# Half of w_out loaded as float32 over SyncE's queue and cast on the chip, with a new order of first loads

## The chip, the core and the metric

The kernel runs on one core of one Trainium2 chip. A core has five engines that work at the same time, each from its own list of instructions: TensorE (PE in the profile; its weight loads are shown as PEld), VectorE (DVE), ScalarE (ACT), GpSimd (POOL) and SyncE (SP). Transfers between the main memory and the on-chip memory (SBUF) are issued by POOL and SP and carried out by 16 DMA engines. Matmul results go to a second on-chip memory, PSUM, and have to be copied out by DVE or ACT.

The metric is the device time of one launch in microseconds (us). The time before is 254.22 us, the median of three runs (253.74, 254.22 and 254.31).

## What is computed

```python
# attention inside chunks of 64 tokens: q, k, v are [8, 8, 576, 64], float32
scores = (q_c @ k_c.T) / sqrt(64)
scores = scores - max(scores)
attn = exp(scores) / (sum(exp(scores)) + 1e-9)
x = (attn @ v_c)                 # put back to [4608, 512]
# feed-forward: w1, w2 [512, 1024], w3 [1024, 1024], w_out [1024, 512], float32
h = ((x @ w1) * (x @ w2)) @ w3
out = h @ w_out                  # [4608, 512], float32
```

## The kernel before

All matmuls are in bfloat16; the inputs are float32 in main memory, and POOL's DMAs cast them while they are loaded. Since no nonlinearity stands between w3 and w_out, the kernel first computes the product w3o = w3 @ w_out on the chip and then applies it as one matrix.

**Groups.** The 4608 tokens are 36 groups of 128 tokens, two chunks each. For a group, q and k are loaded for all heads (`load_qk`, line 264, tile `raw`), transposed (line 317 on PE for groups 0 to 11, line 321 as a DMA transpose on SP's queue, tile `kqT`, for groups 12 to 35), and copied to `kT` and `qd`. Then come the scores (line 345, tile `p_sc`), maximum, subtraction, exponential, sum and normalisation (lines 353 to 371, tiles `nm`, `sd`, `e`, `ss`, `an`), the transpose of the weights (line 376 on PE for groups 0 to 15, line 327 on SP's queue, tile `at`, for the rest), and attn @ v (line 387, tile `p_av`), which is copied into the x tile `xt`. v is loaded for each of the 8 batches (line 270, two DMAs, tile `vd`); a batch has 9 chunks, so that group 4 is the first to need batch 1.

**w3o.** For each of 8 row blocks of w3 (`load_w3`, line 291; shown as `w_sb`): 8 transposes (line 428), a copy (`w3t`), and 8 matmuls with w_out (line 439) in as many pieces as w_out is loaded in: here two halves, blocks 0 to 3 and 4 to 7 (`load_wo`, line 298, tile `wo_sb`). `wo_cut` holds the pieces, `wo_got` what each piece waits for.

**Feed-forward.** Nine tiles of 4 groups (512 tokens). For each of 8 blocks j, 4 matmuls with w1 and 4 with w2 (line 471, `w12` loads at line 282), a copy (`a_sb`) and a product (`abT`); then for each group 8 matmuls with w3o (line 502), a copy to an output row block, and a store on SP's queue (line 512). The first 12 output row blocks reuse the memory of w3 and w_out, the others take the 20 buffers of `o_sb`.

**What sets the order.** The order of instructions on every engine is made when the kernel is built. Each piece of work is an `Op` with the engines that may do it, a planned cost, a key (smaller goes first), what it must come after, and the buffers that it takes and frees. `Plan.run` steps through planned time: whenever an engine is free, it gets the ready op with the smallest key. POOL is the exception: it takes its loads in the order in which they were added, which at the start is the list `LOADS`. ('qk', g) is q and k of group g, ('w3', 7, 8) a row block of w3, ('wo', 4, 8) half of w_out, ('v', 0, 0, 2) v of batch 0, ('w12', 0, 2) the columns for blocks 0 and 1, and ('ident',) the identity matrix that every transpose on PE needs and that POOL makes. For a transfer the plan holds the issuing engine for `issue`, then shares the DMA engines between the first transfers of POOL's and SP's rings, and lets it land `lag` later. So planned costs, planned start times (`free`, `flown`) and lags change no instruction by themselves, but they decide the order on all engines. On the chip the engines wait for each other by semaphores, in that order.

Up to the first `p_av` that isn't a filler, PE gets matmuls on zeros (line 563) where the plan has gaps; 14 of them stand at the very start.

Of the kernel before, what the change touches and what calls it, by code (L numbers as in the profile page):

```python
# [10 lines left out]
ACT = mybir.ActivationFunctionType  # L11
# [3 lines left out]

LOADS = [('wo', 0, 4), ('qk', 1), ('qk', 0), ('ident',), ('w3', 7, 8), ('wo', 4, 8), ('w3', 6, 7), ('qk', 2),
# [3 lines left out]
TILES = [4] * 9  # L22
XT = 16
OUT_AFTER, OUT_KEY = 35, 80
QK_BY_DMA, A_BY_DMA = set(range(12, 36)), set(range(16, 36))

# [18 lines left out]
class Plan:  # L45
# [21 lines left out]

    def run(self):
        free = {e: 0.0 for e in ("PE", "ACT", "DVE", "POOL", "SP")}
        free["POOL"] = free["SP"] = 1.2  # L70
        todo = {e: [] for e in free}
        for i, o in enumerate(self.ops):
            o.place, o.left, o.since = i, len(set(map(id, o.after))), 0.0
# [5 lines left out]
                for e in o.engines:  # L79
                    todo[e].append(o)  # L80

        rings, flown = {"POOL": [], "SP": []}, 3.4
        left, now, order, ends = len(self.ops), 0.0, [], [1.2]
        loads = [o for o in self.ops if "POOL" in o.engines]

        def ended(o):
# [21 lines left out]
        while left or any(rings.values()):  # L108
# [13 lines left out]
            for eng in free:  # L122
                if free[eng] > now or len(rings.get(eng, ())) >= self.RING:
                    continue
                pick = [o for o in (loads[:1] if eng == "POOL" else todo[eng]) if ready(o)]
                if not pick:
                    continue
                o = min(pick, key=lambda o: (o.key, o.place))
                for e in o.engines:
                    todo[e].remove(o)  # L130
                if eng == "POOL":
                    loads.pop(0)
                o.start, o.engine = now, eng
                cost = o.cost[o.engines.index(eng)] if isinstance(o.cost, tuple) else o.cost
                if o.issue:
                    free[eng] = now + o.issue
                    rings[eng].append([free[eng], cost, o])
                else:
                    free[eng] = now + cost
                    o.end = now + cost + o.lag  # L140
                    ended(o)
                for n in o.takes:
                    self.taken[n].append(o)
                order.append(o)
                heapq.heappush(ends, free[eng])
                left -= 1
            while ends and ends[0] <= now:
                heapq.heappop(ends)
# [8 lines left out]
def kernel(  # L157
# [109 lines left out]
    def load_v(b, y0, y1):  # L267
        for t in range(2):
            def emit(eng, t=t):
                nc.gpsimd.dma_start(vds[b % len(vds)][halves[t], 2 * y0:2 * y1, :, t * D:(t + 1) * D].rearrange("p m c d -> p (m c) d"),  # L270
                                    v[b, NM * t + 2 * y0:NM * t + 2 * y1].rearrange("h (c p) d -> p (h c) d", p=C))
            o = load(1.025 * (y1 - y0), 0.5 + 0.335 * (y1 - y0), emit, takes=() if b in v_first else ("vd",),
                     after=(zero_v[b % len(vds)],))
            v_first.setdefault(b, o)
            for y in range(y0, y1):
                v_got.setdefault((b, y), []).append(o)

    def load_w12(j0, j1):
        for dst, w in ((w1_sb, moe_w1), (w2_sb, moe_w2)):
            for t in range(2):  # L280
                def emit(eng, dst=dst, w=w, t=t):
                    nc.gpsimd.dma_start(
                        dst[halves[t], :, j0 * P:j1 * P],
                        w[t * NM * D:(t + 1) * NM * D, j0 * P:j1 * P].rearrange("(m d) n -> d m n", d=D))
                o = load(0.41 * (j1 - j0), 0.62, emit)
        for j in range(j0, j1):
            w12_got[j] = o

    def load_w3(k0, k1):
        def emit(eng):  # L290
            nc.gpsimd.dma_start(w3_sb[:, k0:k1, :], moe_w3.rearrange("(ko p) n -> p ko n", p=P)[:, k0:k1, :])
        o = load(1.45 * (k1 - k0), 0.75, emit)
        for i in range(k0, k1):
            w3_got[i] = o

    def load_wo(k0, k1):
        def emit(eng):
            nc.gpsimd.dma_start(wo_sb[:, k0:k1, :], moe_w_out.rearrange("(ko p) n -> p ko n", p=P)[:, k0:k1, :])
        wo_got.append(load(0.72 * (k1 - k0), 0.75, emit))
        wo_cut.append((k0, k1))  # L300


    x_done = {}

# [117 lines left out]
    def add_w3o(ko, key):  # L422
# [24 lines left out]
        tcp = plan.add(("DVE", "ACT"), (0.7, 1.1), key, tr_copy, after=(tr,), takes=("w3t",), uses=[(tr, "ffn")])  # L447
        mms = []
        for i, (k0, k1) in enumerate(wo_cut):
            mms.append(plan.add("PE", 0.216 * (k1 - k0), key - 0.1 * i, mm_emit(i), after=[tcp, wo_got[i]] + mms,  # L450
                                takes=() if i else ("ffn",), uses=[(tcp, "w3t")], lag=0.2))
        w3o_done.append(plan.add(("ACT", "DVE"), 0.7, key, mm_copy, after=mms, uses=[(mms[0], "ffn")]))

# [69 lines left out]


    made_ident, landing = None, 1.6
    for what, *args in LOADS:
        if what == "ident":
            made_ident = plan.add("POOL", 0.6, 0, lambda eng: make_identity(nc, ident[:]), lag=0.3)
# [67 lines left out]
```

## Time and profile before

| | us |
|---|---|
| median of three runs | 254.22 (253.74 to 254.31) |
| the profiled execution, its own time | 252.69 |
| its span in the profile | 250.9 |
| PE / DVE / ACT / POOL busy | 242.0 / 178.1 / 140.2 / 102.1 |
| POOL's DMA queue | 19.41 MB in 118688 packets |
| SP's DMA queue | 18.36 MB in 41696 packets |

The profile is of one execution, whose own time stands above beside its span; the span leaves out 1.8 us around it. Times in its views count from the span's start. A row of the timeline gives start, duration, engine, line of the kernel, operation, the tile written and the tiles read, and how many instructions it merges; what stands in brackets is the time that the engine was idle before it, and what ended that. DMA rows give the time that the issue took on the engine; when the data had landed is told by a separate line of the view of one source line, in us from the issue. A row of the chain of waits has start, time on the chain, engine, tile and line. A row of the windows has the stretch, its length, the busy time of PE, PEld, DVE, ACT and POOL with counts, the granted PE clock, the DMA engines' share and GB/s. SP's rows are named SPq. MB in DMA rows are bytes written, so a load that casts counts half of what it reads.

### The profile page before, as it was taken

To read this page: it belongs to the slowest core of one execution; us is meant where nothing else is said; L and a number is where in the kernel's file an instruction comes from. 1 tells how busy PE (TensorE), PEld (TensorE's weight loads), DVE (VectorE), ACT (ScalarE), POOL (GpSimd) and SP (SyncE) were. 2 spreads that over 40 slices of the span, in tenths; PEclk is the share of its full clock that TensorE was granted. 3 is DMA by queue.
4 is the path that set the end of the run, shared out by engine and by line. 5 is a ranking of instruction groups with operands and counts; after the bars stand their busy time and mean duration, and the time that the engine had idled before them with its cause. 6 is when DMAs were issued, how large, how long until landed. Compare 5 with 4: busy or idle time off the path is not lost.

```text
span 250.9 us, 4705 instructions
## 1 busy us (share of the span) xinstructions
PE 242.0 (96%) x1771; PEld 124.8 (50%) x1771; DVE 178.1 (71%) x324; ACT 140.2 (56%) x237; POOL 102.1 (41%) x128
## 2 busy tenths in 40 slices
PE   8699989999999999999999999999999999999994
PEld 2356555555655555554544544554454444444443
DVE  6088866888998898788989888888898762232320
ACT  8057465557877786775546556555565344323222
POOL 8847398987529674347414631720000000000000
PEclk9899999999999999999999999999999999999999
DMA  5999999999999999999999999999998992121114
GB/s 79 170 194 190 158 177 180 172 135 144 125 130 154 145 157 133 157 159 126 157 133 155 156 139 157 141 148 151 125 199 280 357 384 80 42 84 42 43 44 167
DMA packets 160406, 38.06 MB, mean 152 GB/s; under 512 B 149376, under 2 KB 154880, under 8 KB 160384
## 3 DMA queue, kind: packets, MB, share of 16 engines
q0 software_dynamic: 118688, 19.41, 119.5%
q1 hardware_dynamic: 41696, 18.36, 40.0%
q8 instruction: 14, 0.23, 0.4%
q14 instruction: 8, 0.07, 0.1%
HBM read 38.80 MB, written 9.44 MB: 192 GB/s over the span
## 4 chain that ended last, share of the span: by engine, by line
PE 87%; DMA 6%; DVE 3%; ACT 2%; issue 1%; POOL 1%; ACTq 0%; POOLq 0%
PE ffn L471 46%; PE ffn L502 23%; PE ffn L439 5%; DMA at<-an 4%; PE p_sc L345 3%; PE p_av L387 3%; DMA raw<-in_k_dram 2%; PE ffn L317 2%; PE p_av L563 1%; PE ffn L376 1%; PE ffn L428 1%; DVE qd L228 1%; ACT kT L226 1%; DVE xt L228 0%; ACT qd L226 0%
## 5 line engine op out<-in xcount | busy, mean ns | idle before, releaser
L471 PE MATMUL ffn<-xt,w_sb 128*128 128x512 bf16 x576 | 134.5, 379 | 0.0
L471 PEld LDWEIGHTS <-w_sb 128*128 128x128 bf16 x576 | 53.6, 98 | 57.6
L480 DVE TENSOR_TENSOR abT<-a_sb,ffn 128x512 bf16<-128x512 f32 x72 | 48.7, 678 | 30.2 <-PE ffn L471 29.6
L502 PE MATMUL ffn<-w3o_sb,abT 128*128 128x512 bf16 (+2 forms) x304 | 67.6, 368 | 0.0
L226 ACT COPY a_sb<-ffn 128x512 f32<-128x512 f32 x72 | 42.0, 584 | 35.7 <-PE ffn L471 35.3
L264 POOL DMA_DIRECT2D raw<-in_q_dram x40 | 34.3, 858 | 31.4 <-DMA kqT<-raw 11.8
L502 PEld LDWEIGHTS <-abT 128*128 128x128 bf16 x304 | 28.4, 98 | 30.5
L264 POOL DMA_DIRECT2D raw<-in_k_dram x40 | 34.3, 859 | 20.8 <-DMA vd<-in_v_dram 10.8
L365 DVE TENSOR_REDUCE ss<-e 128x8 f32<-128x520 bf16 x36 | 24.8, 689 | 5.1 <-ACT e L361 4.8
L361 ACT ACTIVATE e<-sd 128x512 bf16<-128x512 f32 x36 | 22.8, 634 | 7.2 <-DVE sd L357 6.9
L353 DVE TENSOR_REDUCE nm<-p_sc 128x8 f32<-128x512 f32 x36 | 24.3, 675 | 2.4 <-PE p_sc L345 2.3
L226 ACT COPY qd<-kqT 64x512 bf16<-64x512 bf16 x34 | 20.9, 615 | 7.0 <-DMA kqT<-raw 6.7
L357 DVE TENSOR_TENSOR sd<-p_sc,nm 128x512 f32<-128x512 f32 x36 | 24.6, 684 | 0.3
L371 DVE TENSOR_TENSOR an<-e,rs 128x512 bf16<-128x512 bf16 x36 | 24.6, 684 | 0.2
L226 ACT COPY o_sb<-ffn 128x512 f32<-128x512 f32 (+2 forms) x16 | 8.5, 532 | 24.1 <-PE ffn L502 24.0
L270 POOL DMA_DIRECT2D vd<-in_v_dram x16 | 18.5, 1166 | 4.9 <-DMA raw<-in_q_dram 1.7
L226 ACT CAST xt<-p_av 128x512 bf16<-128x512 f32 x24 | 14.0, 585 | 9.3 <-PE p_av L387 9.2
L387 PEld LDWEIGHTS <-vd 128*128 128x128 bf16 x288 | 12.9, 98 | 8.5 <-issue 1.4
L439 PE MATMUL ffn<-wo_sb,w3t 128*128 128x512 bf16 x64 | 15.6, 379 | 0.4 <-DVE w3t L228 0.3
L387 PE MATMUL p_av<-at,vd 128*128 128x64 bf16 x288 | 14.3, 193 | 0.8 <-DVE xt L228 0.7
L345 PEld LDWEIGHTS <-qd 128*128 128x128 bf16 x288 | 12.2, 98 | 5.6 <-ACT qd L226 1.0
L228 DVE COPY qd<-ffn 64x512 bf16<-64x512 bf16 x14 | 5.9, 419 | 10.4 <-ACT kT L226 10.2
(44 smaller groups left out, 160.9 us busy)
## 6 DMA issues: line engine op xcount, KB each, us to landing
out_dram<-o_sb SPq DMA_DIRECT2D x23, 256.0 KB, 2.7
vd<-in_v_dram POOLq DMA_DIRECT2D x16, 288.0 KB, 12.1
raw<-in_q_dram POOLq DMA_DIRECT2D x32, 128.0 KB, 10.0
raw<-in_k_dram POOLq DMA_DIRECT2D x32, 128.0 KB, 9.5
w_sb<-in_moe_w_dram POOLq DMA_DIRECT2D x8, 256.0 KB, 8.8
w_sb<-in_moe_w_dram POOLq DMA_DIRECT2D x16, 128.0 KB, 4.9
out_dram<-w_sb SPq DMA_DIRECT2D x8, 256.0 KB, 3.0
wo_sb<-in_moe_w_out_dram POOLq DMA_DIRECT2D x2, 512.0 KB, 7.1
```

The source lines that it names most:

```text
L226: nc.scalar.copy(o, i)
L264: nc.gpsimd.dma_start(box["t"][r, w], src[b, :, c * C:(c + n) * C, :].rearrange("h p d -> p h d"))
L353: nc.vector.tensor_reduce(nm[:, :, 0], flat(box["sc"]), axis=AX.X, op=ALU.max)
L357: nc.vector.tensor_sub(sd[:], flat(box["sc"]), box["nm"].to_broadcast([P, 8, C]))
L361: nc.scalar.activation(e[:, :, :C], box["sd"][:], ACT.Exp, scale=scale)
L365: nc.vector.reduce_sum(ss[:], box["e"][:], axis=AX.X)
L371: nc.vector.tensor_mul(an[:], box["e"][:, :, :C], box["rs"].to_broadcast([P, 8, C]))
L387: nc.tensor.matmul(t[:, m, cc, :], vds[b % len(vds)][:, m, c, :], box["at"][:, 2 * cc + y, u * C:(u + 1) * C], start=True, stop=True)
L439: nc.tensor.matmul(box["wp"][:], box["t"][:, ki, :], wo_sb[:, ki, :], start=(ki == wo_cut[0][0]), stop=(ki == wo_cut[-1][1] - 1))
L471: nc.tensor.matmul(t[:, :w], wt[:, ki, j * P:(j + 1) * P], x[:, ki, :], start=(ki == 0), stop=(ki == KO - 1))
L480: nc.vector.tensor_mul(box["abT"][:, j, :w], box["as", j][:, :w], box["b", j][:, :w])
L502: nc.tensor.matmul(t[:, :x1 - x0], box["abT"][:, ki, tk * P:(tk + 1) * P], w3o_sb[:, ki, x0:x1], start=(ki == 0), stop=(ki == FO - 1))
```

## The change

The first half of w_out (blocks 0 to 3) is no longer in `LOADS`. A new function `stage_wo` loads it in four pieces of 128 rows (256 KB each) as float32 over SP's queue into `o_sb` buffers, and each is cast into `wo_sb` by ACT or DVE. The first piece of the product with w_out now waits for four casts. The plan's start times are reset (POOL 1.2, SP 0.8, first data at 2.2), a time `reach` is added between the end of an issue and the moment at which its data can flow, and the costs of the v, w1/w2, w3 and w_out loads are a little lower. `LOADS` has a new order.

```diff
-LOADS = [('wo', 0, 4), ('qk', 1), ('qk', 0), ('ident',), ('w3', 7, 8), ('wo', 4, 8), ('w3', 6, 7), ('qk', 2),
-         ('w3', 3, 4), ('w3', 2, 3), ('qk', 3), ('w3', 5, 6), ('w3', 1, 2), ('w3', 0, 1), ('v', 0, 0, 2), ('qk', 4),
-         ('w3', 4, 5), ('w12', 0, 2), ('qk', 5), ('w12', 6, 8), ('w12', 2, 4), ('qk', 6), ('w12', 4, 6), ('qk', 7),
-         ('qk', 8), ('v', 1, 0, 2), ('qk', 9), ('qk', 10)]
+LOADS = [('qk', 0), ('w3', 7, 8), ('w3', 3, 4), ('qk', 1), ('w3', 0, 1), ('wo', 4, 8), ('w3', 1, 2), ('ident',),
+         ('qk', 2), ('w3', 2, 3), ('w3', 5, 6), ('qk', 3), ('w3', 6, 7), ('qk', 5), ('qk', 4), ('v', 0, 0, 2), ('w3', 4,
+         5), ('w12', 0, 2), ('qk', 6), ('w12', 4, 6), ('qk', 7), ('w12', 2, 4), ('w12', 6, 8), ('qk', 8), ('v', 1, 0, 2),
+         ('qk', 9), ('qk', 10)]
+STAGED = 4
...
-        free["POOL"] = free["SP"] = 1.2
+        free["POOL"], free["SP"] = 1.2, 0.8
...
-        rings, flown = {"POOL": [], "SP": []}, 3.4
-        left, now, order, ends = len(self.ops), 0.0, [], [1.2]
+        rings, flown, reach = {"POOL": [], "SP": []}, 2.2, {"POOL": 1.6, "SP": 1.3}
+        left, now, order, ends = len(self.ops), 0.0, [], [0.8, 1.2]
...
-                    rings[eng].append([free[eng], cost, o])
+                    rings[eng].append([free[eng] + reach[eng], cost, o])
...
+                if o.issue:
+                    heapq.heappush(ends, rings[eng][-1][0])
...
-            o = load(1.025 * (y1 - y0), 0.5 + 0.335 * (y1 - y0), emit, takes=() if b in v_first else ("vd",),
+            o = load(1.0 * (y1 - y0), 0.5 + 0.335 * (y1 - y0), emit, takes=() if b in v_first else ("vd",),
...
-                o = load(0.41 * (j1 - j0), 0.62, emit)
+                o = load(0.36 * (j1 - j0), 0.62, emit)
...
-        o = load(1.45 * (k1 - k0), 0.75, emit)
+        o = load(1.42 * (k1 - k0), 0.75, emit)
...
-        wo_got.append(load(0.72 * (k1 - k0), 0.75, emit))
+        wo_got.append([load(0.68 * (k1 - k0), 0.75, emit)])
...
+    def stage_wo(k0, k1):
+        staged = []
+        for ki in range(k0, k1):
+            box = {}
+
+            def emit(eng, ki=ki, box=box):
+                box["t"] = sb("o_sb", [P, D_MODEL], f32)
+                nc.sync.dma_start(box["t"][:], moe_w_out[ki * P:(ki + 1) * P])
+
+            def cast(eng, ki=ki, box=box):
+                copy(eng, wo_sb[:, ki, :], box["t"][:])
+
+            o = plan.add("SP", 0.67, -2000 + ki, emit, takes=("o_sb",), lag=1.6, issue=0.1)
+            staged.append(plan.add(("ACT", "DVE"), 0.6, -1500 + ki, cast, after=(o,), uses=[(o, "o_sb")]))
+        wo_got.append(staged)
+        wo_cut.append((k0, k1))
...
-            mms.append(plan.add("PE", 0.216 * (k1 - k0), key - 0.1 * i, mm_emit(i), after=[tcp, wo_got[i]] + mms,
+            mms.append(plan.add("PE", 0.216 * (k1 - k0), key - 0.1 * i, mm_emit(i), after=[tcp] + wo_got[i] + mms,
...
+    if STAGED:
+        stage_wo(0, STAGED)
```

In the changed build, ACT does all four casts, right behind its two zero copies of `vd`, and SP's four loads are its first instructions. From POOL, the loads come in the order of the new list. The order of matmuls, of the at and kqT turns on SP, and of the copies is a new one on the whole length of the kernel; PE, DVE, ACT and SP do the same work as before beside the staged half and two fewer fillers.

## The prediction

> **What bounds the kernel now.** I read the page first, then the chain of waits, then who waited for whom, and last the timeline of the first 40 us and of the DMA queues' later stretches.
>
> ```profile
> span 250.9 us, 4705 instructions
> PE 242.0 (96%) x1771; PEld 124.8 (50%) x1771; DVE 178.1 (71%) x324; ACT 140.2 (56%) x237; POOL 102.1 (41%) x128
> PE 87%; DMA 6%; DVE 3%; ACT 2%; issue 1%; POOL 1%; ACTq 0%; POOLq 0%
> ```
>
> TensorE is busy for 96% of the span and carries 87% of the chain, so the kernel ends when TensorE has worked off its fixed list. A change gains only by starting that list earlier or by taking waits out of it. The timeline shows where it isn't yet useful work:
>
> ```profile
> 1.26 0.89 POOL L298 DMA_DIRECT2D wo_sb<-in_moe_w_out_dram  x1 [0.81 <-POOLq L580]
> ...
> 2.03 4.12 ACT L241 COPY vd<-nought 128x2304 f32<-128x2304 f32 x2
> 2.14 0.90 POOL L264 DMA_DIRECT2D raw<-in_q_dram  x1
> 3.02 0.90 POOL L264 DMA_DIRECT2D raw<-in_k_dram  x1
> ...
> 5.62 0.27 POOL masks.py:197 MEMSET ident<- 128x128 bf16 x1
> 5.96 0.29 POOL masks.py:199 TENSOR_SCALAR_AFFINE_SELECT ident<-ident 128x128 bf16<-128x128 bf16 x1
> 6.20 0.57 POOL L291 DMA_DIRECT2D w_sb<-in_moe_w_dram  x1
> 6.76 0.75 POOL L298 DMA_DIRECT2D wo_sb<-in_moe_w_out_dram  x1
> ...
> 9.17 0.62 PE L317 MATMUL ffn<-ident,raw 128*128 128x128 bf16 x8 [2.03 <-DMA raw<-in_k_dram]
> ...
> 16.82 0.58 ACT L226 CAST w3o_sb<-ffn 128x512 bf16<-128x512 f32 x1 [0.22 <-PE ffn L439]
> ...
> 38.61 1.89 PE L471 MATMUL ffn<-xt,w_sb 128*128 128x512 bf16 x8
> ```
>
> The first transposes wait until 9.17 us for q and k, which stand behind the first half of w_out on POOL's queue. The first FFN matmul comes at 38.61 us. In between, the weights and inputs arrive as fast as the DMA engines deliver:
>
> ```profile
> 0.00:5.00 5.00, 3.81 (x9) 1.34 (x10) 3.54 (x6) 4.25 (x3) 3.94 (x9) 1.00 0.36 48
> 5.00:10.00 5.00, 2.97 (x16) 1.26 (x15) 0.25 (x3) 1.16 (x1) 4.92 (x9) 1.00 2.02 168
> ```
>
> The last column is GB/s: 168 once the stream flows, 48 in the first 5 us. 48 x 5 = 240 KB at 168 KB/us is 1.4 us of flow, so the stream is dead for the first 3.6 us.
>
> **What the change removes and adds.** L298's first issue (0.89 us of POOL, 0.5 MB written as bfloat16) goes. SyncE, idle until its first transposed load far behind, issues four float32 loads of 256 KB, and ScalarE casts them: its order in the changed build is table load, two zero copies, four casts, first kT copy. The zero copies end at 2.03 + 4.12 = 6.15 us, and four casts at 0.58 us (the row of the same shape; its source is PSUM, here SBUF) end at 8.5 us. The first kT copy can come only after the first transposes, so the 2.3 us are hidden; without that cover they would cost the kT copy up to 2.3 us. The four staging tiles come from the 20 of the output rows and are free some 180 us before those are taken: nothing.
>
> **The start of TensorE.** POOL now issues q and k of group 0 at once, then two w3 blocks, q and k of group 1, a w3 block, the second half of w_out, another w3 block, and only then the identity: four raw loads at a pitch of 0.88 us (2.14 to 3.02), four w3 at 0.57, one at 0.75, together 6.6 us from 1.26. The identity's start moves from 5.62 to 7.8 us and its end from 6.25 to 8.4 us. Group 0's data land before that (at worst the stream carries 0.52 + 0.26 MB first, 4.6 us at 168 KB/us), so the identity replaces the load as the last wait: first transposes at about 8.5 us, 0.7 us earlier.
>
> **The lead of the loads, L.** How much earlier does everything on POOL's stream land? A load of the same size and type as the new ones, on SyncE's queue in the other direction, and the load that goes:
>
> ```profile
> L512 SPq DMA_DIRECT2D out_dram<-o_sb x1: 332/332/332, 207.9 to 207.9; - x1
> ...
> DMA to landing us min/median/max: 2.0/2.0/2.0
> ...
> L298 POOL DMA_DIRECT2D wo_sb<-in_moe_w_out_dram x1: 888/888/888, 1.3 to 1.3; - x1
> ...
> DMA to landing us min/median/max: 6.0/6.0/6.0
> ```
>
> One SyncE transfer on a quiet chip lands 2.0 us after its issue, the first POOL load 6.0 us after. SyncE can issue at about 0.8 us (ScalarE's and POOL's first rows lie at 0.7 to 1.3 us), so its bytes may flow from about 2.1 us, and 3.6 - 2.1 = 1.5 us of the dead time is used. Bounds: nothing at all, if SyncE's bytes only push POOL's aside; and 3.1 us, if all 0.52 MB (0.52 / 0.168) travel beside the rest. I take **L = 1.5 us**, the dead time, since the rows on either side of it (48 and 168 GB/s) are the nearest.
>
> The Trainium skill, "DMA: Bandwidth & Descriptors", section "Issuing engines are not separate DMA queues", speaks against the change: DMAs of all issuers run on the same 16 DMA engines, and a second issuer saves only issue time. In the rows of the start POOL is the only issuer, so no run here shows it yet. By that rule L would be no more than the issue time of 0.89 us, and the sum nothing.
>
> **Who spends the lead.** TensorE's order is fixed when the kernel is built, and the changed build asks for several loads earlier in its list. For each such place I take the slack before (start less landing), the shift in matmul work in front of it, and L. The work is counted with three steps of the chain of waits, in which matmuls follow each other without a gap:
>
> ```profile
> 40.50 0.45 PE ffn L317 x8
> ...
> 42.90 0.23 PE p_sc L345 x8
> 43.13 5.18 PE ffn L471 x24
> ```
>
> Eight transposes take 0.45 us, eight scores 0.23, and eight matmuls of 512 columns a third of 5.18, 1.73 us.
>
> First FFN matmul. It needs four w1/w2 loads, the last of them here:
>
> ```profile
> L282 POOL DMA_DIRECT2D w_sb<-in_moe_w_dram x2: 612/614/617, 30.7 to 31.3; - x2
> ...
> DMA to landing us min/median/max: 4.6/4.7/4.7
> ```
>
> It lands at 31.3 + 4.7 = 36.0, slack 2.6 us. The new list puts one more q/k pair in front (two raw loads, 1.8 us) and one more group's transposes and scores (0.45 + 0.23 us) ahead of the matmul: it could gain 2.6 - 1.8 + 0.7 + L = L + 1.5 = 3.0 us. Not the bound.
>
> Group 4's p_av, the first to need v of batch 1:
>
> ```profile
> L270 POOL DMA_DIRECT2D vd<-in_v_dram x2: 1202/1210/1219, 47.0 to 48.2; - x2
> ...
> DMA to landing us min/median/max: 8.2/8.8/9.3
> 58.38 0.40 PE L387 MATMUL p_av<-at,vd 128*128 128x64 bf16 x8
> ```
>
> v lands at 48.2 + 9.3 = 57.5, slack 0.9 us. In the changed build the eight output matmuls ahead of it (1.73 us) stand behind it and four transposes (0.22 us) ahead: 1.5 us earlier in the list, while the same loads precede v. It can gain L + 0.9 - 1.5 = L - 0.6 us; a TensorE that is further ahead waits here, with the output matmuls queued behind.
>
> The middle, where SyncE's transposes feed p_av:
>
> ```profile
> 116.16 1.57 SPq L327 DMA_TRANSPOSE at<-an  x1
> 117.90 6.01 SPq L321 DMA_TRANSPOSE kqT<-raw  x2
> ...
> L327 SPq DMA_TRANSPOSE at<-an x1: 1571/1571/1571, 116.2 to 116.2; - x1
> ...
> DMA to landing us min/median/max: 7.9/7.9/7.9
> 124.93 0.40 PE L387 MATMUL p_av<-at,vd 128*128 128x64 bf16 x8
> L321 SPq DMA_TRANSPOSE kqT<-raw x1: 3595/3595/3595, 117.9 to 117.9; - x1
> ...
> DMA to landing us min/median/max: 10.9/10.9/10.9
> ...
> 173.37 1.24 SPq L327 DMA_TRANSPOSE at<-an  x1
> ...
> DMA to landing us min/median/max: 9.4/9.4/9.4
> 182.80 0.39 PE L387 MATMUL p_av<-at,vd 128*128 128x64 bf16 x8
> ```
>
> Group 19's at lands at 116.2 + 7.9 = 124.1, slack 0.8 us. In the changed order of SyncE it stands behind group 23's kqT turn (117.90 + 3.60 = 121.5), 5.3 us later, and its p_av stands 3.7 us later in the list (eight FFN and eight output matmuls at 1.73, one score of 0.23): 0.8 + 3.7 - 5.3 = -0.8, a gain of L - 0.8 us at most. Group 29's at lands at 173.4 + 9.4 = 182.8, exactly when its p_av starts: slack 0.0. SyncE's order around it is unchanged, and four FFN matmuls (0.86 us) fewer stand ahead: L - 0.9 us. Both assume that the lead of the first loads carries on to the middle, where the loads wait for each other's buffers and not for TensorE.
>
> **The sum.** The smallest of these is L - 0.9 = **0.6 us** of gain; the rest of the early gain is given back in waits before p_av. Against the profiled execution that is 252.69 - 0.6 = 252.1 us (span 250.3 with the same 1.8 us around it). That execution lies 1.5 us under the median of the runs shown, 254.22; the same gain on the median gives **253.6 us**. By the bounds of L: 0.9 us lost (255.1) to 2.2 us gained (252.0). Planned costs and start times emit no instruction; they act through the orders alone.
>
> **Rivals.** *The middle doesn't bind:* the at turns come as early as TensorE does, and only v of batch 1 and the first FFN matmul limit: between 0.9 and 3.0 us of gain, 2.0 in the middle, **252.2 us**. For it: a TensorE that is busy for 96% of the span waits little there now. Against it: group 29's slack of nothing.
>
> *No lead:* SyncE's float32 bytes only displace POOL's. L is 0 to 0.3, and the earlier demands cost 0.6 to 0.9 us: **255.0 us**. For it: the stream is at its full 168 GB/s right behind its start. Against it: the dead 3.6 us. This is where the Trainium skill's rule on shared engines, cited above, leads.
>
> *SyncE's head of line:* an at turn behind a kqT turn that itself waits for a load. If it lands after 10.9 us, as the kqT row of 117.90 does, and not after 7.9, group 19's p_av is short by 0.8 + 3.0 - 1.5 = 2.3 us: **256.5 us**. It decides from a landing 0.7 us over the old one; against it, the other at rows here land after 7.9 and 9.4.
>
> *The change does nothing to the end:* late casts or a late identity hold TensorE where the loads held it: 254.2 us.
>
> **Chances.** Forecast (gain 0.2 to 1.1) 0.38; middle not binding 0.20; no lead 0.22; head of line 0.15; nothing 0.05. What this measurement can tell from no change is about 0.2%, 0.5 us. Of the forecast 0.22 lies over that: faster 0.42; same 0.16 + 0.05 = 0.21; slower 0.37. The range takes the bounds of L and a part of the head-of-line case: 251.9 to 255.7; the forecast's own is 253.1 to 254.0.
>
> **What would show it.** Right: the identity's select ending at 8.3 to 8.6 us and the first transposes just behind it; the casts done by 9 us; the first FFN matmul before 37 us; p_av of group 4 waiting for v, which lands at 55.5 to 56.5; p_av of groups 18, 19, 24 or 29 waiting for at. Wrong: v of batch 1 landing at 57 us or later (L was nothing) or under 55; TensorE without waits between 60 and 200 us (the middle doesn't bind); waits of over 1.5 us there (head of line).

## The result, and the profile after

| | before | after | ratio |
|---|---|---|---|
| first comparison, 15 executions each | 254.31 us (252.99 to 256.85) | 251.67 us (250.12 to 254.07) | 0.9888 [0.9852, 0.9925] |
| second, 29 and 12 | 253.87 | 252.06 (249.63 to 254.99) | 0.9909 [0.9874, 0.9943] |
| third, 31 and 8 | 254.08 | 251.93 (250.20 to 253.41) | 0.9922 [0.9885, 0.9959] |

Medians are over all executions; the ratios leave out those more than 1.5% above the fastest of their kernel. The change makes the kernel faster by 1.8 to 2.6 us, about 0.9%. The forecast was 0.6 us. The table also shows that one program's executions spread over 3 to 5 us, so a single profile says little about differences of one microsecond.

The page of the changed kernel (its profiled execution took 252.69 us, by chance the same as the one of before) begins with the span and the busy times; the third line is the summary of the chain of waits, the last a row of the DMA issues (count, KB each, median us from issue to landing):

```profile
span 250.9 us, 4671 instructions
...
PE 239.3 (95%) x1737; PEld 125.3 (50%) x1769; DVE 173.8 (69%) x315; ACT 146.3 (58%) x250; POOL 101.4 (40%) x127
...
PE 76%; DMA 16%; POOL 3%; issue 3%; DVE 1%; ACT 1%; POOLq 0%
...
o_sb<-in_moe_w_out_dram SPq DMA_DIRECT2D x4, 256.0 KB, 3.9
```

TensorE is still the bound. DMA stands in the chain with 16% instead of 6%: more of the chain now runs through landings. The row of the DMA issues holds the four new transfers. At 256 KB each they write 1.05 MB, twice what the bfloat16 half wrote.

The timeline of the first 10 us, after, without the fillers and memsets:

```profile
0.74 1.82 SPq L313 DMA_DIRECT2D o_sb<-in_moe_w_out_dram  x4
...
1.25 1.01 POOL L267 DMA_DIRECT2D raw<-in_q_dram  x1 [0.81 <-POOLq L602]
...
2.26 0.89 POOL L267 DMA_DIRECT2D raw<-in_k_dram  x1
...
6.06 1.65 ACT L229 CAST wo_sb<-o_sb 128x512 bf16<-128x512 f32 x3
...
7.91 0.62 ACT L229 CAST wo_sb<-o_sb 128x512 bf16<-128x512 f32 x1 [0.19 <-DMA o_sb<-in_moe_w_out_dram]
8.40 0.55 POOL L294 DMA_DIRECT2D w_sb<-in_moe_w_dram  x1 [1.09 <-DMA raw<-in_q_dram]
...
9.24 0.29 POOL masks.py:199 TENSOR_SCALAR_AFFINE_SELECT ident<-ident 128x128 bf16<-128x128 bf16 x1
...
9.58 0.80 PE L337 MATMUL ffn<-ident,raw 128*128 128x128 bf16 x8 [2.62 <-POOL ident masks.py:199]
```

And the stretches of 0 to 5 and 5 to 10 us (last column GB/s, 48 and 168 before):

```profile
0.00:5.00 5.00, 3.81 (x9) 1.34 (x10) 3.54 (x6) 4.25 (x3) 3.95 (x9) 1.00 0.54 160
5.00:10.00 5.00, 2.38 (x13) 1.12 (x12) 0.25 (x3) 3.33 (x5) 3.83 (x8) 0.98 1.43 188
```

The dead time at the start is used. The casts end at 8.53 us as forecast. The identity, though, comes 1.1 us late: POOL had issued eight transfers and stood still until q of group 0 had landed. The first transposes start at 9.58 us, 0.4 us later than before.

Who waited for whom, after, on TensorE (us in total, times, longest):

```profile
PE ffn L337 <- POOL ident masks.py:199: 2.6, 1, 2.6
PE p_av L407 <- DMA vd<-in_v_dram: 1.7, 2, 1.3
...
PE p_av L407 <- DMA at<-an: 0.2, 1, 0.2
```

p_av waits for v now, 1.7 us, as forecast. It hardly waits for at, which the forecast had as the limit.

### The profile page after: what moved, and what is told of

Its sections match the earlier page's. It is cut to its first block, busy times and chain, and to the rows that moved or that the text cites. A ratio compares the mean times of both kernels' runs of the same rounds, so it can differ in the third digit from the quotient of the medians.

```text
span 250.9 us, 4671 instructions
## 1 busy us (share of the span) xinstructions
PE 239.3 (95%) x1737; PEld 125.3 (50%) x1769; DVE 173.8 (69%) x315; ACT 146.3 (58%) x250; POOL 101.4 (40%) x127
## 4 chain that ended last, share of the span: by engine, by line
PE 76%; DMA 16%; POOL 3%; issue 3%; DVE 1%; ACT 1%; POOLq 0%
PE ffn L491 41%; PE ffn L522 23%; DMA vd<-in_v_dram 7%; DMA at<-an 4%; PE p_av L407 3%; PE p_sc L365 3%; DMA raw<-in_q_dram 3%; DMA raw<-in_k_dram 2%; PE ffn L459 2%; PE ffn L337 1%; PE p_av L585 1%; POOL raw L267 1%; POOL vd L273 1%; PE ffn L396 1%; PE ffn L448 1%
## 5 line engine op out<-in xcount | busy, mean ns | idle before, releaser
L491 PE MATMUL ffn<-xt,w_sb 128*128 128x512 bf16 x555 | 131.6, 379 | 1.1
L522 PE MATMUL ffn<-w3o_sb,abT 128*128 128x512 bf16 (+2 forms) x298 | 66.8, 368 | 0.4
L229 ACT COPY o_sb<-ffn 128x512 f32<-128x512 f32 (+2 forms) x20 | 10.8, 542 | 29.4 <-PE ffn L522 29.3
L229 ACT COPY qd<-kqT 64x512 bf16<-64x512 bf16 x37 | 22.7, 614 | 2.7 <-DMA kqT<-raw 2.4
L229 ACT CAST xt<-p_av 128x512 bf16<-128x512 f32 x27 | 15.8, 586 | 10.1 <-PE p_av L407 9.9
L285 POOL DMA_DIRECT2D w_sb<-in_moe_w_dram x16 | 9.9, 629 | 2.2 <-DMA vd<-in_v_dram 0.8
```

What stands on the lines that cost most here:

```text
L229: nc.scalar.copy(o, i)
L491: nc.tensor.matmul(t[:, :w], wt[:, ki, j * P:(j + 1) * P], x[:, ki, :], start=(ki == 0), stop=(ki == KO - 1))
L522: nc.tensor.matmul(t[:, :x1 - x0], box["abT"][:, ki, tk * P:(tk + 1) * P], w3o_sb[:, ki, x0:x1], start=(ki == 0), stop=(ki == FO - 1))
```

## Ten profiles of the two kernels

No single profile settles the question, so both kernels were profiled several times. Here is how one row of the table comes about. For v of batch 1 the view of its line gives the two issues and the time to landing; the later issue plus the longer time is the landing (changed kernel, the earliest of its six executions, then the latest):

```profile
L273 POOL DMA_DIRECT2D vd<-in_v_dram x2: 1174/1182/1189, 45.9 to 47.1; - x2
...
DMA to landing us min/median/max: 7.4/7.8/8.2
```

```profile
L273 POOL DMA_DIRECT2D vd<-in_v_dram x2: 1172/1180/1189, 47.6 to 48.8; - x2
...
DMA to landing us min/median/max: 8.2/8.8/9.4
```

So v lands at 55.3 and 58.2 us. The end of the second FFN tile is the start of its last product abT, in the timeline of the same two executions:

```profile
81.23 0.69 DVE L500 TENSOR_TENSOR abT<-a_sb,ffn 128x512 bf16<-128x512 f32 x1 [0.23 <-PE ffn L491]
```

```profile
84.27 0.68 DVE L500 TENSOR_TENSOR abT<-a_sb,ffn 128x512 bf16<-128x512 f32 x1
```

The landing of group 29's at and the start of its p_av come from the same views. Three rows are of experiments told below; their place beside the two kernels is what matters here.

| profiled execution (its time) | v of batch 1 | second tile ends | at of 29 | p_av of 29 | span |
|---|---|---|---|---|---|
| before (252.69) | 57.5 | 83.4 | 182.8 | 182.8 | 250.9 |
| before, again (253.89) | 57.9 | 83.0 | 183.8 | 184.0 | 252.1 |
| before, third (253.89) | 59.5 | 84.6 | 183.6 | 184.0 | 252.1 |
| before, fourth (253.86) | 58.9 | 84.1 | 183.7 | 184.0 | 252.1 |
| old order, half over SyncE (252.55) | 57.3 | 82.4 | 182.6 | 182.9 | 250.8 |
| the same, again (252.82) | 57.0 | 82.1 | 182.8 | 183.2 | 251.0 |
| after (252.69) | 57.5 | 83.5 | 179.2 | 182.2 | 250.9 |
| after, again (251.95) | 57.0 | 83.0 | 178.7 | 181.1 | 250.2 |
| after, third (252.36) | 56.5 | 82.5 | 180.7 | 181.9 | 250.6 |
| after, fourth (251.86) | 55.3 | 81.2 | 178.3 | 181.4 | 250.1 |
| after, fifth (253.91) | 58.2 | 84.3 | 181.5 | 183.4 | 252.1 |
| after, sixth (251.64) | 56.6 | 82.6 | 178.8 | 181.1 | 249.8 |
| new order, half over POOL (252.80) | 57.7 | 83.7 | 180.1 | 182.0 | 251.0 |

Two regularities can be read off. In the **new order** the second tile ends 25.9 to 26.1 us behind the landing of v in every row, and TensorE waits 0.2 to 1.7 us for v in each of the six profiles of the changed kernel: v sets the start there. Behind it, at of 29 always lands 1.2 to 3.1 us ahead of its p_av. In the **old order** the second tile ends 25.1 or 25.2 us behind v (25.9 in the one execution that the forecast was made from, where v had 0.9 us to spare). There, at of 29 lands within 0.4 us of its p_av in all six rows, and the span ends 68.1 to 68.5 us behind that landing. With the half over SyncE, v lands at 57.3 and 57.0 instead of 57.5 to 59.5, and the second tile ends 1.5 us earlier than in the mean of before (82.2 against 83.8). But at of 29, at 182.6 and 182.8, lands only 0.8 us earlier (183.5 in the mean), and the span ends 0.9 us earlier: the old order's middle gives part of the lead back.

The transfer of this at is another regularity. From issue to landing it takes 9.0 to 9.5 us in the six rows of the old order and 7.2 to 7.7 us in the seven of the new one (8.2 in the version without the half, told below). It is also issued earlier: at 172.0 us in the mean of the six profiles of after, 174.2 in the four of before.

## The experiments

Each kernel is compared with the one before on the same chip. The diffs are short forms of the edits.

**The two kernels again.** No edit.

> The changed kernel once more, for a second profile and a second set of times. 0.985 to 0.993 of before again. Its first profile (252.69 us, in the upper half of its runs) had no lead: v of batch 1 landed at 57.5 us as before, and TensorE waited 1.3 us for it. If a faster execution (250 to 251 us) is one in which the loads land earlier, then in a profile of such a one v lands at 55 to 56.5 us and that wait is gone or shorter; if not, v lands at 57.5 again and the time was won in the middle.

> The kernel before once more, for a second profile. All theories: within the spread of its fifteen runs, 253.0 to 256.9 us. If the first profile of it (252.69 us, below all fifteen) caught an execution with unusually early loads, this one has v of batch 1 landing later than 57.5 us and TensorE waits before 60 us that the first did not have; if the loads do not differ between executions, v lands at 57.5 us again.

Measured: 252.06 us, ratio 0.9909 [0.9874, 0.9943], profiled at 251.95 with v at 57.0 and 0.9 us of waits for it; an execution of 250 to 251 us wasn't caught. Before was profiled at 253.89, with v at 57.9, little later than 57.5. The waits of this second profile of before, on TensorE:

```profile
PE ffn L317 <- DMA raw<-in_k_dram: 1.7, 1, 1.7
PE p_av L387 <- DMA at<-an: 1.3, 2, 0.7
```

The waits of p_av for at, hidden in the first profile of before, are 1.3 us here. The forecast saw an execution that hardly showed them.

**The order alone.** The changed kernel with the half on POOL's queue, ahead of everything, and no casts:

```diff
             def emit(eng, ki=ki, box=box):
-                box["t"] = sb("o_sb", [P, D_MODEL], f32)
-                nc.sync.dma_start(box["t"][:], moe_w_out[ki * P:(ki + 1) * P])
+                if ki == k0:
+                    nc.gpsimd.dma_start(wo_sb[:, k0:k1, :], moe_w_out.rearrange("(ko p) n -> p ko n", p=P)[:, k0:k1, :])
 
             def cast(eng, ki=ki, box=box):
-                copy(eng, wo_sb[:, ki, :], box["t"][:])
+                pass
```

> All orders of the changed kernel, but the first half of w_out comes as one casting DMA at the head of POOL's queue, as before, and nothing is cast on ScalarE. Theory path (the gain is the lead of the loads by SyncE's queue): 0.998 to 1.006 of before, and v of batch 1 lands later than in the changed kernel by 0.9 us or more. Theory order (the gain is the new order of the engines, the path is worth nothing): 0.985 to 0.993 as with the change, and the same landing.

Measured: 252.92 us (252.58 to 254.85), ratio 0.9973 [0.9945, 1.0001]. Its profile waits 2.3 us for v and not at all for at:

```profile
PE ffn L337 <- POOL ident masks.py:199: 3.6, 1, 3.6
PE p_av L407 <- DMA vd<-in_v_dram: 2.3, 2, 1.6
```

The order by itself is worth about 0.3%, with an interval that just reaches no change. That is just under what the theory "path" expected (0.998 to 1.006) and outside of "order" (0.985 to 0.993); v lands 0.85 us later than in the mean of the changed kernel.

**The path alone.** The kernel before, its orders kept, with the half over SyncE and the casts on ScalarE behind the zero copies:

```diff
         def emit(eng):
-            nc.gpsimd.dma_start(wo_sb[:, k0:k1, :], moe_w_out.rearrange("(ko p) n -> p ko n", p=P)[:, k0:k1, :])
+            if k0:
+                nc.gpsimd.dma_start(wo_sb[:, k0:k1, :], moe_w_out.rearrange("(ko p) n -> p ko n", p=P)[:, k0:k1, :])
+                return
+            for ki in range(k0, k1):
+                t = sb("o_sb", [P, D_MODEL], f32)
+                nc.sync.dma_start(t[:], moe_w_out[ki * P:(ki + 1) * P])
+                staged.append((ki, t))
...
             o.emit(o.engine)
+            if o is zero_v[2]:
+                for ki, t in staged:
+                    nc.scalar.copy(wo_sb[:, ki, :], t[:])
```

> All orders of the kernel before, but the first half of w_out comes by SyncE's queue as four float32 loads and is cast by ScalarE behind its two zero copies. Theory path: 0.985 to 0.995 of before, since group 1's q and k land 1 to 2 us earlier and everything behind follows. Theory order: 0.997 to 1.003; the first transposes start earlier, but the old order has no use for it.

> The kernel before with its own orders and half of w_out over SyncE's queue, for one more profile (250.5 to 253.6 us so far, profiled at 252.6). If it is caught at about 251: 'v decides' expects v of batch 1 before 56.5 us and the second FFN tile's end before 81.5 us; 'middle or tail' expects 82.5 us there and waits for at of under 0.5 us instead of 1.1.

Measured: 252.79 us, ratio 0.9929 [0.9892, 0.9966]; the execution profiled once more took 252.82 us. The theory "path" expected 0.985 to 0.995, "order" 0.997 to 1.003: "path" holds. Of a lead of 1.3 us at v (mean 57.15 against 58.45 in the four profiles of before) 0.9 is left in the span (250.9 against 251.8). Both profiles wait 1.0 to 1.1 us for at. Since no execution near 251 us was caught, the two theories for the second profile stay undecided. Path and order, 0.7% and 0.3%, add up to the change's 0.8 to 1.1%, within intervals of 0.3 to 0.4% each.

**p_av later in the old order.** The kernel before, with the p_av of groups 19, 27, 28 and 29 behind two more blocks of matmuls each:

```diff
-        for o in plan.run():
+        ops = plan.run()
+        for g in (19, 27, 28, 29):
+            i = ops.index(avs[g])
...
+            moved = [av] + [x_done[g]] * (ops.index(x_done[g]) < j)
+            rest = [o for o in ops if o not in moved]
+            i = rest.index(ops[j]) + 1
+            ops = rest[:i] + moved + rest[i:]
+        for o in ops:
```

> The kernel before, in which p_av of groups 19, 27, 28 and 29 and its copy stand behind two more blocks of matmuls; nothing else is moved. Theory middle (the kernel before loses its time in waits of p_av for at around these groups, and the new order has slack there): 0.993 to 0.998 of before, and the waits of p_av for at, 0.6 to 1.3 us in two profiles, are gone. Theory path alone: 0.999 to 1.002.

Measured: 255.24 us, ratio 1.0057 [1.0028, 1.0087], slower. The waits for at are gone, and others have taken their place:

```profile
PE p_sc L345 <- ACT o_sb L226: 1.2, 1, 1.2
PE p_sc L345 <- ACT qd L226: 1.2, 3, 0.5
```

Group 29's at now lands 3.6 us ahead of its p_av (184.25 and 187.84 us), but the waits have moved to p_sc, behind copies by ScalarE. Both expectations missed, the one of the theory that the middle binds and the one of no change; since the edit added waits of its own, it is no clean test of either.

**The planned times alone.** The changed kernel planned with the old start times and costs (the whole plan runs again):

```diff
-        free["POOL"], free["SP"] = 1.2, 0.8
+        free["POOL"] = free["SP"] = 1.2
...
-        rings, flown, reach = {"POOL": [], "SP": []}, 2.2, {"POOL": 1.6, "SP": 1.3}
+        rings, flown, reach = {"POOL": [], "SP": []}, 3.4, {"POOL": 0.0, "SP": 0.0}
```

> The changed kernel with the planned costs and start times of the kernel before; the staged half and the new list of loads stay, the orders on all engines are planned anew. If the reset times make the orders good: 0.994 to 1.004 of before, with waits in the middle like those of the kernel before. If the list and the staged half do it: 0.988 to 0.994, as with the whole change.

Measured: 251.66 us, ratio 0.9912 [0.9874, 0.995]. The new times bring nothing that can be measured: the list and the staged half do it, as the second expectation had it. The one execution that was profiled took 895.83 us, so no waits are read from it.

**The old list.** The changed kernel with the old sequence of loads, without the first half of w_out (again with a new plan):

```diff
-LOADS = [('qk', 0), ('w3', 7, 8), ('w3', 3, 4), ('qk', 1), ...
+LOADS = [('qk', 1), ('qk', 0), ('ident',), ('w3', 7, 8), ('wo', 4, 8), ...
```

> The changed kernel with the old list of loads (without the staged half); the staged half and the reset times stay. If the new list does it: 0.994 to 1.000 of before (the path alone gave 0.993 with the old order). If reset times and staged half do it: 0.988 to 0.993. No wait for v of batch 1 like the 0.9 to 1.7 us of the changed kernel, if that wait comes from asking for it earlier.

Measured: 260.52 us, ratio 1.0262 [1.0224, 1.03]. TensorE waits for raw and v at the start and for sd:

```profile
PE ffn L337 <- DMA raw<-in_k_dram: 2.3, 4, 1.4
PE p_av L407 <- DMA vd<-in_v_dram: 1.6, 1, 1.6
...
PE p_sc L365 <- DVE sd L377: 1.2, 1, 1.2
```

Both expectations missed. The plan was made anew for this list, so it isn't a plan that doesn't fit its list: with the staged half and the new start times, the old list is 2.6% slower than before, and the new one 0.9% faster. Which of the waits costs this isn't shown.

**The half left out.** The changed kernel without these loads; the first half of w_out is zero in this run:

```diff
-                box["t"] = sb("o_sb", [P, D_MODEL], f32)
-                nc.sync.dma_start(box["t"][:], moe_w_out[ki * P:(ki + 1) * P])
+                pass
...
-                copy(eng, wo_sb[:, ki, :], box["t"][:])
+                nc.scalar.copy(wo_sb[:, ki, :], nought.to_broadcast([P, D_MODEL]))
```

> The changed kernel without the load of the first half of w_out, which is zeros from ScalarE instead: this part of the product is left out. It shows what the half still costs the other loads on SyncE's queue. Theory displaced (the float32 bytes only push POOL's aside): group 0's k lands 2 us or more earlier than the 8.5 to 9.0 us of the changed kernel, and v of batch 1 at 54 to 55.5 us. Theory dead time (the half travels mostly before POOL's data flow): k of group 0 0.5 to 1.3 us earlier, v of batch 1 at 56 to 57 us. The time: 0.980 to 0.990 by the first, 0.986 to 0.992 by the second.

Measured: 251.55 us, ratio 0.9911 [0.9875, 0.9947], what the change itself gives. The first q lands 3.6 us behind its issue and the first k 5.4; in the six profiles of the changed kernel it is 6.0 to 7.0 for q and 5.9 to 6.8 for k. The view of q's and k's line, first in the changed kernel (two pairs, its first profile), then in this one (the first pair):

```profile
L267 POOL DMA_DIRECT2D raw<-in_q_dram x2: 938/974/1010, 1.3 to 4.2; - x2
...
DMA to landing us min/median/max: 6.7/7.5/8.1
```

```profile
L267 POOL DMA_DIRECT2D raw<-in_q_dram x1: 1007/1007/1007, 1.3 to 1.3; - x1
L267 POOL DMA_DIRECT2D raw<-in_k_dram x1: 893/893/893, 2.3 to 2.3; - x1
...
DMA to landing us min/median/max: 3.6/4.5/5.4
```

But v of batch 1 lands no earlier (47.2 + 9.6 = 56.8 us, against a mean of 56.85):

```profile
L273 POOL DMA_DIRECT2D vd<-in_v_dram x2: 1174/1182/1189, 46.1 to 47.2; - x2
...
DMA to landing us min/median/max: 8.7/9.2/9.6
```

So the half on SyncE's queue delays the first q by 2.4 to 3.4 us and the first k by 0.5 to 1.4, and nothing of it can be seen at v, in one profile of a kernel whose v moves by 3 us. k at 7.7 us, v at 56.8 and the ratio are what the theory "dead time" expected. By the end nothing can be told from not loading the half at all, within the 0.9 us of the interval.

**More profiles of the changed kernel.** Three, for an execution near 250 us.

> The changed kernel again, for the profile of one more execution. Its times spread from 249.6 to 254 us, and the two profiles so far are of executions of 252.0 and 252.7. If an execution at about 250 is caught, theory 'v decides': v of batch 1 lands about 2 us earlier than the 57.0 to 57.5 of those two, the wait before the p_av of group 4 is under 0.5 us, and the second FFN tile ends at about 81.5 us instead of 83.0 to 83.5. Rival 'middle or tail': v lands as before and the second tile ends at 83, and the 2 us are gained behind it.

> The same kernel and the same two theories as for the first look: at about 250 us the second FFN tile ends at 81.5 us ('v decides') or at 83 ('middle or tail'). At 252 to 254 us both expect waits before p_av of 1 to 2.5 us for v.

> The same kernel and the same two theories as for the first look: at about 250 us the second FFN tile ends at 81.5 us ('v decides') or at 83 ('middle or tail'). At 252 to 254 us both expect waits before p_av of 1 to 2.5 us for v.

Measured: 252.36, 251.86 and 253.91 us; none was near 250. The second of them has the earliest v and the second tile's end at 81.2 us, as "v decides" asks. The rest of it shows a second place, in its timeline of TensorE:

```profile
123.42 0.39 PE L407 MATMUL p_av<-at,vd 128*128 128x64 bf16 x8 [1.64 <-ACT wo_sb L229]
```

The copy it is put down to ends at 123.36 and is a copy of an output row that p_av doesn't read. Group 18's at, in the view of its line, lands at 113.6 + 9.7 = 123.3 us:

```profile
L347 SPq DMA_TRANSPOSE at<-an x1: 2048/2048/2048, 113.6 to 113.6; - x1
...
DMA to landing us min/median/max: 9.7/9.7/9.7
```

Where TensorE is early, it loses 1.6 of the 2.3 us (83.5 - 81.2) here. In the other five profiles of the changed kernel the same at lands 0.1 to 0.7 us ahead of its p_av, and TensorE waits up to 0.4 us for it: behind v, this is the next place with nothing to spare. In the new order it is issued right behind the turn of group 22; in the four profiles of before it had 0.7 to 1.4 us to spare.

**The two places.** First, SyncE turns at of 18 and 19 ahead of kqT of 22 and 23:

```diff
+        for g in (18, 19):
+            i, j = ops.index(turns[g + 4]), ops.index(ats[g])
+            ops.insert(j, ops.pop(i))
```

> The changed kernel, with SyncE's at turns of groups 18 and 19 ahead of the kqT turns of groups 22 and 23. Theory 'two gates' (v of batch 1 first, at of group 18 second): at of 18 lands at about 118 to 120 us instead of 123 to 125, its p_av never waits; executions in which v comes late (57 us and later) gain nothing, those in which it comes early gain up to 1.6 us: median 0.3 to 0.8 us under the changed kernel's on the same chip. Rival 'v alone': no difference (within 0.3 us). Rival 'SyncE's head of line': the kqT turns now late make the p_sc of 22 and 23 wait, 0.5 us slower or more.

Second, the p_av of group 4 behind the first eight output matmuls:

```diff
+        at0, to = ops.index(avs[4]), min(ops.index(o) for o in firsts)
+        moved = [avs[4]] + [x_done[4]] * (ops.index(x_done[4]) < to)
+        rest = [o for o in ops if o not in moved]
+        i = rest.index(ops[to]) + 1
+        for o in rest[:i] + moved + rest[i:]:
```

> The changed kernel, with the p_av of group 4 behind the first eight output matmuls instead of ahead of them, right in front of group 5's. 'Two gates': the second FFN tile ends 24.9 to 25.1 us behind the landing of v instead of 26.0 (1.73 us less behind it, 0.6 us more for one p_av buffer used twice in a row), and of these 0.9 to 1.1 us the at of group 18 takes a part: 0.3 to 0.8 us faster in the median. 'v alone': 0.9 to 1.1 us faster. Rival 'the load stream as a whole, not v' (w1/w2 pieces and raw tiles just as late as v): no difference.

Both, and the changed kernel beside them:

> Both edits. 'Two gates': the gains add up or more, 1.0 to 1.6 us under the changed kernel's median; 'v alone': as with the second edit alone, 0.9 to 1.1 us; 'load stream as a whole': as with the first alone.

> The changed kernel itself, on the same chip as the three. Both theories: 251.6 to 252.1 us median, ratio 0.989 to 0.992 to the kernel before, v of batch 1 between 55.3 and 58.2 us and the end of the second FFN tile 26.0 us behind it.

| | median | ratio to before |
|---|---|---|
| at first | 252.26 | 0.9925 [0.9893, 0.9956] |
| p_av of 4 late | 251.98 | 0.9921 [0.9890, 0.9951] |
| both | 251.43 | 0.9911 [0.9879, 0.9943] |
| the changed kernel | 251.93 | 0.9922 [0.9885, 0.9959] |

In the first, group 18's at is issued at 110.9 and lands 8.1 us later:

```profile
L347 SPq DMA_TRANSPOSE at<-an x1: 1196/1196/1196, 110.9 to 110.9; - x1
...
DMA to landing us min/median/max: 8.1/8.1/8.1
```

That is 119.0 us, 3.3 ahead of its p_av. The waits for at are gone from that profile, and its execution (250.83 us, span 249.1) is the fastest that was profiled: v lands at 56.0, and 167.1 us follow the second tile's end, where the early execution above, with v at 55.3, took 168.8. Its median, however, isn't lower. In the second the tile ends 25.5 us behind v (56.6 and 82.1), half of what was expected of it. With both edits TensorE no longer waits for v, which lands at 48.5 + 8.8 = 57.3 us:

```profile
L273 POOL DMA_DIRECT2D vd<-in_v_dram x2: 1182/1190/1197, 47.3 to 48.5; - x2
...
DMA to landing us min/median/max: 7.8/8.3/8.8
```

```profile
58.20 0.40 PE L407 MATMUL p_av<-at,vd 128*128 128x64 bf16 x8
59.27 0.39 PE L407 MATMUL p_av<-at,vd 128*128 128x64 bf16 x8 [0.67 <-ACT xt L229]
```

The tile still ends at 83.3 us, no earlier than the changed kernel's mean of 82.85. In this profile what comes before v keeps TensorE nearly as late, as the rival "load stream as a whole" says. That rival expected no difference from the second edit and none is seen; "two gates" missed its medians for all three edits and "v alone" for the second and third. No ratio can be told from the changed kernel's: in single executions both places show, for the median neither is shown to matter.

**The kernel before, twice more.** Two more profiles.

> The kernel before, for one more profile. Its second FFN tile ended at 83.0 and 83.4 us, 25.1 and 25.9 us behind the landing of v of batch 1, and from there to the last matmul it took 164.1 and 165.7 us. 'The old order loses it in the middle': at 254 us or more, the second tile ends by 83.5 and the stretch behind it takes 165.5 us or more, with waits for at of 1 us or more in all. 'The stream loses it at the start': v of batch 1 lands at 58.5 us or later, the second tile ends at 84 or later, and 164 to 165 us follow.

> The same kernel and the same two theories, for one more execution: the second FFN tile's end by 83.5 us and 165.5 us or more behind it (middle), or 84 us or later and 164 to 165 us behind it (start).

Measured: 253.89 and 253.86 us. v lands at 59.5 and 58.9, the second tile ends at 84.6 and 84.1, and the TensorE work behind takes 164.1 and 164.6 us (its last matmul ends at 248.7 in both). These are the numbers of "the start". The earlier profile of 253.89 us, with 83.0 and 165.7, has those of "the middle": the same time comes about in two ways. v in the first of the two, and TensorE's wait for it:

```profile
L270 POOL DMA_DIRECT2D vd<-in_v_dram x2: 1202/1210/1219, 48.1 to 49.3; - x2
...
who waited for it (us, times):
  PE p_av L387: 1.5, 1
...
DMA to landing us min/median/max: 9.1/9.7/10.2
```

## Why the forecast was wrong

**The lead of the loads** was right. v of batch 1 lands at a mean of 58.45 us in four profiles of before and 56.85 in six of after: L is 1.6 us where 1.5 was forecast (1.3 with the old order, 0.85 within the new one), known to half a microsecond or so with such spreads. Its make-up was less right. No run shows the 1.3 us from SyncE's issue to its first bytes that stand in the forecast's 2.1 us: in three profiles with the half on SyncE's queue the DMA engines first move data between 1.6 and 1.8 us. And 168 GB/s was no limit for SyncE's loads: the changed kernel's stream reaches 369 GB/s from 2.5 to 3.0 us. The first profile of after alone would have said that L is nothing, 57.5 against 57.5; the prediction itself named "57 us or later" as the sign. That comparison was one early execution of before with a late one of after.

The Trainium skill, "DMA: Bandwidth & Descriptors", section "Issuing engines are not separate DMA queues", allowed the second issuer no more than the issue time that it saves, here 0.89 us. The means of the traces, 0.85 to 1.6 us, lie around and above that; with executions 2 us apart they don't decide whether it is exceeded. They speak against the rival that the forecast made of it, in which the lead is 0 to 0.3 us: as long as the half stood on POOL's queue, in either order, v never landed before 57.5 us in six profiles.

**The start** was wrong and cost nothing. The forecast had POOL issue without a stop and counted 0.52 MB of SyncE's ahead of the first q. There are 1.05 MB; the first q and k land 5.9 to 7.0 us behind their issues, and POOL stands still for 0.3 to 1.2 us. The identity comes at 8.7 to 9.6 instead of 8.4 us, the first transposes at 8.75 to 9.69 in six profiles, and the first FFN matmul at 38.1 to 39.8 instead of before 37. Without the half they come at 8.5 and 36.95 us, and the median is no better. The casts are hidden, as forecast. (The staging tiles are free some 125 us, not 180, before the first output row goes into such a buffer, at 133.6 us before the change; that, too, cost nothing.)

**Group 4's p_av** was right: it waits for v, and its cap of L - 0.6 = 0.9 us is what the second tile's end shows, 83.8 before and 82.85 after in the mean. The parts were a little different. In the forecast 0.9 us of slack stood against 1.5 us of earlier demand; in three of four profiles of before there is no slack, and the second tile ends 26.0 us behind v instead of 25.3 in the mean, so that 0.7 of the 1.6 us is lost.

**Group 19's at** was right in place, not in weight. It goes out behind group 23's kqT turn. In the first profile it lands as its p_av starts:

```profile
117.08 1.92 SPq L341 DMA_TRANSPOSE kqT<-raw  x1
119.05 3.48 SPq L347 DMA_TRANSPOSE at<-an  x1
```

```profile
129.21 0.41 PE L407 MATMUL p_av<-at,vd 128*128 128x64 bf16 x8 [0.23 <-DMA at<-an]
```

The landing behind the turn took 10.1 us here, 2.2 more than the 7.9 of before and beyond the 0.7 us from which the rival "SyncE's head of line" was to decide; the issue at 119.05, not 121.5, kept it at a wait of 0.23 us. In the other five profiles it took 7.3 to 7.6 us four times and 9.3 once, and waits for it were no longer. So the gain of 0.7 us that the forecast gave it was no cap. The at that has nothing to spare is group 18's, behind the turn of group 22, where the forecast didn't look.

**Group 29's at is the step that failed:** "SyncE's order around it is unchanged, and four FFN matmuls (0.86 us) fewer stand ahead: L - 0.9 us". The order is unchanged, but the times are not. The step let the landing come earlier by L, 1.5 us, and took the time from issue to landing as it was. In the timeline after, the turn goes out at 171.97 us instead of 173.37, right behind two kqT turns that start at 165.80 instead of 167.01:

```profile
165.80 6.07 SPq L341 DMA_TRANSPOSE kqT<-raw  x2
171.97 1.52 SPq L347 DMA_TRANSPOSE at<-an  x1
```

```profile
DMA to landing us min/median/max: 7.2/7.2/7.2
```

```profile
182.23 0.40 PE L407 MATMUL p_av<-at,vd 128*128 128x64 bf16 x8
```

It lands 7.2 us behind its issue instead of 9.4, so at 179.2, 3.0 us ahead of the p_av. In the means of six and four profiles the landing comes 4.0 us earlier (179.5 instead of 183.5), not 1.5: 2.2 us by the earlier issue and 1.7 by the shorter transfer (7.5 instead of 9.25). With 4.0 instead of 1.5 this term is 3.1 us of gain and no cap. Why the transfer is shorter in the new order is **open**. What the step saw was real for the old order, where this at lands within 0.4 us of its p_av in all six profiles; it was carried over to an order in which it no longer holds. At this at the rival "the middle doesn't bind", forecast at 252.2 us with a chance of 0.20, is right; at group 18's it is not.

**The sum.** Without the caps of groups 29 and 19 that of group 4 is the smallest, and the same working gives 0.9 instead of 0.6 us and 253.3 us on the median. So the step that failed explains 0.3 us of the miss and no more. The profiles show 1.2: 0.9 at the second tile's end and 0.25 behind it (the spans end 168.0 us behind it before and 167.8 after, in the mean), and the mean spans are 251.8 and 250.6. The right base was the median, as chosen: 252.69 was an early execution. The medians show 1.8 to 2.6 us. The 0.6 to 1.4 us between the two stay **open**: executions at about 250 us (8 of the changed kernel's 35 took 250.4 us or less) were never caught in a profile, and four and six executions drawn from spreads of 4 us fix each mean to half a microsecond or so. The low end of the range, 251.9, was missed by 0.2 us in the first comparison and held in the other two.

## What to carry to other kernels

A slack of zero that is read in one order is no cap for another, even where the instructions around it keep their order: here the transfer was issued 2.2 us earlier and took 1.7 us less. Look for the places that the new order itself leaves without slack (here group 18's at). Take the bound from several profiles where one is to be had for each: here v's landing moves by 2 to 3 us from execution to execution, more than the effect. Moving the path alone, with all orders kept, gave 0.7% of the 0.8 to 1.1%; the old list of loads under the new settings, with the plan made anew, cost 2.6%.

## What the runs showed of the hardware that wasn't expected

- POOL stopped after eight transfers, for 0.3 to 1.2 us in six profiles (1.09 in the first), and went on when q of group 0 had landed. No run shows whether the chip or the semaphores of the program held it.
- With 1.05 MB on SyncE's queue the first q lands 2.4 to 3.4 us later and the first k 0.5 to 1.4, yet v of batch 1, nearly 50 us on, lands no later than without these bytes (56.85 in the mean of six profiles against 56.8 in one).
- The same program's v lands between 55.3 and 58.2 us, and the 26 us of work behind it then repeat to 0.1 us.
- The same DMA transpose (group 29's at), right behind two kqT turns in both orders, lands 9.0 to 9.5 us after its issue in six profiles of the old order and 7.2 to 7.7 us in seven of the new one (8.2 without the half). Why isn't shown.
